# A convolution and mixture-of-experts kernel: four pairs of chunks routed together, small routing steps moved between engines, load orders fixed

## The chip, the cores and the metric

The kernel runs on one core of a Trainium2 chip. The metric is the device time of one execution in microseconds. A core has TensorE (PE: matrix products, with PEld for loading weights), VectorE (DVE), ScalarE (ACT), GpSimd (POOL) and SyncE (SP, which issues most DMA transfers here; GpSimd issues the scattered ones). Each engine runs its own list of instructions in order, and semaphores join the lists.

## The reference

```python
# x: 8 x 3584 x 192, weight_gen: 8 x 3584 x 8 heads x 7 taps, 8 experts, F = 1024
w = softmax(weight_gen, axis=-1)                       # seven taps for each row and head
y[s, head] = sum(w[s, head, k] * x_padded[s + k, head] for k in range(7))
x = y.reshape(28672, 192)
logits = x @ w_gate                                    # 28672 x 8
e = argmax(logits); g = softmax(logits)[e]
out[row] = g[row] * (relu(x[row] @ w1[e]) @ w2[e])     # each row through one expert
```

## The kernel before

The 28672 rows are cut into 28 chunks of 1024 (8 rows on each of 128 partitions). A chunk goes through these stages.

- **Convolution** (`taps`, lines 415 to 438, through `tap_ops`). VectorE multiplies the input by each of seven tap weights and adds up: seven products (`tv`, line 386) and six sums (`acc`, line 410) of 128 x 1536. For the first five chunks TensorE does the sums.
- **Split** (`high`, `low`). Each float32 row becomes a high and a low float16 part, written with its row number into a payload tile `pl` (three of them). TensorE transposes it for the gate.
- **Routing** (`finish`, lines 722 to 733). `logits` on TensorE into the PSUM tile `pm`; `route1` on VectorE (sum of the two halves `lg`, maximum, difference, one-hot `oh`; ScalarE's Exp gives `eg`); `ranks` on TensorE; `gate` (sum `se`, product with `rsx`, reciprocal into the payload); `places` (the position `pos` of each row in its expert's queue). `send` scatters the 8 rows per partition with 8 indirect DMAs of GpSimd into a queue in device memory.
- **Choice** (`choose`, `select`). As soon as a chunk is routed, a plan made ahead (`make_plan`, `t_main`) says how many tiles may be taken. `select` finds the fullest queues with seven steps on VectorE over a 1 x 72 table (`free`, `key`, `key`, `top`, `rows`, `key`, `room`). `rows` holds where each tile starts. SyncE reads it into a register.
- **Experts** (`fetch`, `experts`, `l2`). A tile has 256 rows up to chunk 4, then 384, and 128 at the end. `fetch` loads `xt` (a transposing DMA from the queue, which waits until the scatters of its chunk have landed), `wt` (the expert's weights, 1796 KB) and `meta`. For each of 8 groups TensorE makes `ph` with five matmuls (line 890), ScalarE takes the ReLU's high half `hh` (line 910), and VectorE the low half `hl` (line 913). For some tiles (those chosen up to chunk `SUBS - 1`, and every eighth from chunk 18 on) TensorE subtracts `hh` itself (line 903) and ScalarE writes `hl` (line 905). The second layer of the tile before (line 787) is mixed in between; ScalarE scales its output `o` (line 791) and GpSimd scatters it to `out`.

Tiles are numbered in the order of the choice: 0 to 13 have 256 rows, 14 is chunk 5's only tile, 15 to 17 are chunk 6's, 18 and 19 chunk 7's, and so on (31 to 33 chunk 12's, 34 and 35 chunk 13's, 47 chunk 18's first, 70 chunk 26's last).

The order of VectorE's list is written out by the program: `vector_step` (lines 1027 to 1064) keeps one clock for VectorE and one for TensorE, built from costs in the text, and puts out whatever is due: a low half, a weight step, a routing step, a split, else the next tap. A routing step that yields is due again `STEP` = 0.2 us later, so one tap usually falls between two steps. The lists of the other engines are ordered by a scheduler from what depends on what, with routing preferred. The PSUM pool of `ph` has 4 buffers, `o` has 6, `wt` 3, `xt` 3.

Of the kernel before, what the change touches and what calls it, by code (L numbers as in the profile page):

```python
# [47 lines left out]
HOLD = 6  # L48
CAPS = (128, 128, 128, 128, 112, 96, 80, 64, 48, 32)
# [4 lines left out]
FETCH = 16.0  # L54
W_AT = 10.0
# [64 lines left out]
def conv_moe_kernel(ctx: ExitStack, tc: tile.TileContext, x, wgen, w_gate, w1, w2, out):  # L120
# [43 lines left out]
    revE = const.tile([P, J, E], F32, name="revE")  # L164
    nc.gpsimd.iota(revE, pattern=[[0, J], [-1, E]], base=E, channel_multiplier=0,
# [7 lines left out]
    oh_t = []  # L173
    for i in range(2):
        t = const.tile([P, J + 1, E], F16, name=f"oh{i}")
        nc.gpsimd.memset(t, 0.0)
        oh_t.append(t)
    eg_t = []
    for i in range(2):
        t = const.tile([P, J, E + 1], F32, name=f"eg{i}")  # L180
        nc.gpsimd.memset(t[:, :, E:], 1e-9)
        eg_t.append(t)
# [270 lines left out]
    def scale(c):  # L453
        k = ch[c]
        ssq = rt.tile([P, 1], F32, name="ssq")
        nc.vector.tensor_reduce(ssq, ssqs, axis=AX.XY, op=ALU.add)  # L456
        yield 0.1
        ssi = rt.tile([P, 1], I32, name="ssi")
        nc.vector.tensor_scalar(ssi, ssq.bitcast(I32), 24, 23, op0=ALU.logical_shift_right,
                                op1=ALU.arith_shift_left)  # L460
        yield 0.1
        k.rsx = rt.tile([P, 1], F32, name="rsx", bufs=4)
# [49 lines left out]
    def logits(c):  # L512
        k = ch[c]
        k.pm = ps_m.tile([P, 512], F32, name="pm")
        k.lp = k.pm[:, 0:J * 2 * E].rearrange("p (j t e) -> p j t e", j=J, t=2)
        for j in range(J):
            for n in range(3):
                nc.tensor.matmul(k.lp[:, j], k.xg[:, 3 * j + n, :], gw[:, n], start=(n == 0), stop=(n == 2))  # L518
                clock[1] += GATE

    def route1(c):
        k = ch[c]
        k.lg = rt.tile([P, J, E], F32, name="lg")
        k.eg = eg_t[c % 2]
        nc.vector.tensor_reduce(k.lg, k.lp.rearrange("p j t e -> p j e t"), axis=AX.X, op=ALU.add)
        yield STEP
        lm = rt.tile([P, J], F32, name="lm")
        nc.vector.tensor_reduce(lm, k.lg, axis=AX.X, op=ALU.max)
        yield STEP
        nc.vector.tensor_tensor(k.lg, k.lg, lm.unsqueeze(2).to_broadcast([P, J, E]), op=ALU.subtract)  # L530
        nc.scalar.activation(k.eg[:, :, 0:E], k.lg, AF.Exp, scale=k.lsc)
        yield STEP
        pri = rt.tile([P, J, E], F32, name="pri")
        nc.vector.scalar_tensor_tensor(pri, k.lg, 0.0, revE, op0=ALU.is_ge, op1=ALU.mult)
        yield STEP
        pmx = rt.tile([P, J], F32, name="pmx")
        nc.vector.tensor_reduce(pmx, pri, axis=AX.X, op=ALU.max)
        yield STEP
        k.oh = oh_t[c % 2]
        nc.vector.tensor_tensor(k.oh[:, 0:J, :], pri, pmx.unsqueeze(2).to_broadcast([P, J, E]), op=ALU.is_equal)  # L540

    def ranks(c):
        k = ch[c]
        k.rp = k.pm[:, 256:256 + (J + 1) * E].rearrange("p (j e) -> p j e", j=J + 1)
        nc.tensor.matmul(k.rp, tri, k.oh, start=True, stop=False)
        for j in range(J):
            nc.tensor.matmul(k.rp[:, j + 1:, :], ones_h, k.oh[:, j:j + 1, :].to_broadcast([P, J - j, E]),
                             start=False, stop=(j == J - 1))
        clock[1] += 0.3

    def gate(c):
        k = ch[c]
        se = rt.tile([P, J], F32, name="se")
        nc.vector.tensor_reduce(se, k.eg, axis=AX.X, op=ALU.add)
        yield STEP
        nc.vector.tensor_tensor(se, se, k.rsx.to_broadcast([P, J]), op=ALU.mult)
        yield STEP
        nc.vector.reciprocal(k.pl.bitcast(F32)[:, :, D], se)
        yield STEP

    def places(c):
        k = ch[c]
        rk = rt.tile([P, J, E], F32, name="rk")
        bs = base[-1]
        nc.vector.tensor_tensor(rk, k.rp[:, 0:J, :], bs.unsqueeze(1).to_broadcast([P, J, E]), op=ALU.add)
        nb = rt.tile([P, E], F32, name="nb", bufs=3)
        nc.vector.tensor_tensor(nb, k.rp[:, J, :], bs, op=ALU.add)
        base.append(nb)
        yield STEP
        nc.vector.tensor_tensor(rk, rk, k.oh[:, 0:J, :], op=ALU.mult)  # L570
        yield STEP
        k.pos = rt.tile([P, J], I32, name="pos")
        with nc.allow_low_precision("queue positions are whole numbers below 2**24"):
            nc.vector.tensor_reduce(k.pos, rk, axis=AX.X, op=ALU.add)
        yield STEP

    def send(c):
        k = ch[c]
        for j in range(J):
# [18 lines left out]
    def select(T, S_, rows):  # L598
# [4 lines left out]
        nc.vector.tensor_tensor(free, room.unsqueeze(2).to_broadcast(sh), steps[T], op=ALU.add)  # L603
        yield STEP
# [10 lines left out]
        nc.vector.tensor_scalar(rows, top, -1.0, float(TOP), op0=ALU.mult, op1=ALU.add)  # L615
# [53 lines left out]
    first_ = []  # L669
    sent = [0]  # L670
# [123 lines left out]
    def fetch(n):  # L794
# [36 lines left out]
        rows_of(m)  # L831
        if n == 0:
# [6 lines left out]
    def experts():  # L839
# [25 lines left out]
        while True:  # L865
# [13 lines left out]
            for t in range(groups):  # L879
# [16 lines left out]
                if ((n % 8 == 1 and todo[n][3] >= LATE_SUBS) or todo[n][3] < SUBS) and todo[n][3] < NCH - 3:  # L896
# [236 lines left out]
```

## Time and profile before

| | |
|---|---|
| median of 3 runs | 1186.94 us (1186.53 to 1188.32) |
| profiled execution | 1185.47 us |
| its span, first to last instruction | 1183.8 us |
| mean granted TensorE clock | 0.991 |

The profile shows one execution. Busy times are the sums of listed durations; a matmul's end is modelled, and listed durations of neighbours can overlap. A wait is put down to the instruction whose semaphore came last.

### The profile page before, as it was taken

How to read it: one execution, taken by the hardware profiler on the slowest of the kernel's cores; microseconds unless marked ns; L12 is line 12 of the kernel's file. 1: busy time of each engine (PE TensorE's matmuls, PEld its weight loads, DVE VectorE, ACT ScalarE, POOL GpSimd, SP SyncE). 2: the span in 40 equal slices, each digit the busy share in tenths (PEclk: the TensorE clock that was granted, in tenths of full speed). 3: DMA queues.
4: the chain of work that ended last, by engine and by line, in shares of the span. 5: the costliest groups of instructions: out<-in, count | busy, mean ns of one | idle time of the engine just before them, and what ended most of it. 6: DMA issues, size and time to landing. Idle time of an engine off the chain costs nothing. (4 is left out here: it accounts for less than half of the span.)

```text
span 1183.8 us, 29289 instructions
## 1 busy us (share of the span) xinstructions
PE 1123.8 (95%) x11327; PEld 913.1 (77%) x11327; DVE 1034.9 (87%) x1771; ACT 647.1 (55%) x1348; POOL 696.3 (59%) x633
## 2 busy tenths in 40 slices
PE   5689799999999999999999999999999999999996
PEld 3455489998778878787788888787777777778996
DVE  7999999999999999999999999999999997833231
ACT  3555477777556555545554555656465556443342
POOL 7998647766654654664566566447555675721222
PEclk9999899999999999999999999999999999999999
DMA  9989899999889787888898788777687666799993
GB/s 280 378 299 335 248 335 308 307 307 307 254 219 279 239 257 229 258 240 232 221 290 237 209 276 260 234 209 236 235 242 245 196 151 223 235 330 353 351 344 136
DMA packets 182847, 311.44 MB, mean 263 GB/s; under 512 B 131243, under 2 KB 154785, under 8 KB 167470
## 3 DMA queue, kind: packets, MB, share of 16 engines
q1 hardware_dynamic: 160702, 264.17, 73.3%
q0 software_dynamic: 22000, 45.33, 12.0%
q8 instruction: 91, 1.49, 0.5%
q14 instruction: 54, 0.44, 0.1%
HBM read 226.97 MB, written 60.45 MB: 243 GB/s over the span
## 5 line engine op out<-in xcount | busy, mean ns | idle before, releaser
L890 PE MATMUL ph<-xt,wt 128*128 128x384 f16 (+6 forms) x3680 | 571.2, 296 | 9.5 <-DVE hl L913 5.5
L787 PE MATMUL yo<-wt,hh 128*128 128x192 f16 (+1 forms) x3648 | 489.8, 246 | 2.9 <-ACT o L791 2.9
L589 POOL DMA_INDIRECT out_dram<-o,meta x228 | 281.1, 1233 | 323.5 <-ACT o L791 254.5
L787 PE MATMUL yo<-wt,hl 128*128 128x192 f16 (+1 forms) x1824 | 438.3, 246 | 0.0
L890 PEld LDWEIGHTS <-wt 128*128 128x128 f16 x3680 | 317.7, 98 | 124.3 <-issue 6.4
L910 ACT ACTIVATE hh<-ph 128x384 f16<-128x384 f32 (+2 forms) x485 | 238.5, 495 | 292.9 <-PE ph L890 272.1
L913 DVE SCALAR_TENSOR_TENSOR hl<-ph,hh 128x384 f16<-128x384 f32 (+2 forms) x485 | 260.4, 552 | 110.7 <-ACT hh L910 110.2
L787 PEld LDWEIGHTS <-hh 128*128 128x128 f16 (+1 forms) x3648 | 330.2, 98 | 32.9 <-issue 3.7
L589 POOL DMA_INDIRECT queue<-pl,pos x224 | 289.7, 1293 | 98.6 <-issue 72.9
L386 DVE TENSOR_TENSOR tv<-x_sb,wp 128x1536 f32<-128x1536 f32 (+1 forms) x173 | 286.2, 1656 | 1.7 <-PE ph L395 1.4
L410 DVE TENSOR_TENSOR acc<-acc,tv 128x1536 f32<-128x1536 f32 x138 | 239.6, 1736 | 0.0
L787 PEld LDWEIGHTS <-hl 128*128 128x128 f16 (+1 forms) x1824 | 178.7, 98 | 18.5 <-ACT hl L905 0.2
L791 ACT ACTIVATE o<-yo,fac 128x192 f32<-128x192 f32 (+1 forms) x228 | 90.5, 418 | 89.5 <-PE yo L787 85.1
L508 ACT ACTIVATE xg<-ph 128x1024 f16<-128x1024 f16 x84 | 81.6, 1022 | 38.2 <-PE ph L506 38.0
L395 PE MATMUL ph<-tv,identf 128*128 128x384 f32 x210 | 82.6, 539 | 17.8 <-DVE tv L386 17.1
L395 PEld LDWEIGHTS ph<-tv,identf 128*128 128x128 f32 x210 | 41.4, 209 | 45.2 <-DVE tv L386 19.0
L899 ACT ACTIVATE hh<-ph 128x512 f16<-128x512 f32 (+1 forms) x88 | 48.9, 562 | 22.1 <-PE ph L890 16.0
L447 ACT ACTIVATE junk<-x_sb 128x768 bf16<-128x768 f32 (+2 forms) x56 | 48.0, 857 | 16.1 <-DVE ssq L456 6.0
L905 ACT ACTIVATE hl<-ph 128x512 f16<-128x512 f32 (+1 forms) x88 | 47.7, 559 | 10.6 <-PE ph L903 10.2
L506 PE MATMUL ph<-idh,pl 128*128 128x128 f16 x672 | 52.3, 219 | 0.4 <-DVE pl L500 0.3
L486 ACT ACTIVATE pl<-acc 128x768 f16<-128x768 f32 (+1 forms) x51 | 39.0, 805 | 15.3 <-DVE acc L410 9.2
L506 PEld LDWEIGHTS <-pl 128*128 128x128 f16 x672 | 42.7, 98 | 5.9 <-ACT pl L491 2.6
(133 smaller groups left out, 768.9 us busy)
## 6 DMA issues: line engine op xcount, KB each, us to landing
wt<-wq SPq DMA_DIRECT2D x92, 1796.0 KB
x_sb<-in_x_dram SPq DMA_DIRECT2D x27, 1344.0 KB
w_sb<-in_weight_gen_dram SPq DMA_DIRECT2D x28, 224.0 KB
wq<-ws SPq DMA_DIRECT2D x8, 772.0 KB
f<-in_moe_w_dram SPq DMA_DIRECT2D x8, 768.0 KB
f<-in_moe_w_dram SPq DMA_DIRECT2D x8, 512.0 KB
wq<-ws SPq DMA_DIRECT2D x8, 512.0 KB
wq<-ws SPq DMA_DIRECT2D x32, 128.0 KB
```

Of the source, the lines that this page charges most:

```text
L386: eng.tensor_tensor(out, xs, ws, op=ALU.mult)
L395: nc.tensor.matmul(ap[:, 0:m], identf, tf[:, 2 * i * D:2 * i * D + m], start=(n == 0), stop=(n == KW - 1))
L410: eng.tensor_tensor(ac, ac, t, op=ALU.add)
L506: nc.tensor.transpose(pt[:, m, :], p16[:, j, n * P:(n + 1) * P], idh)
L508: nc.scalar.activation(k.xg[:, i:i + 8, :], pt, AF.Copy)
L589: st = nc.gpsimd.indirect_dma_start(out=dst, out_offset=bass.IndirectOffsetOnAxis(ap=idx, axis=0), in_=src, in_offset=None, **kw)
L787: nc.tensor.matmul(y, hx[:, f, sl], w2v[:, f, t, :], start=(f == 0 and k == 0), stop=(f == NF - 1 and k == 2))
L791: nc.scalar.activation(o[0:m, :], y, AF.Copy, scale=fac[0:m, s:s + 1])
L890: nc.tensor.matmul(ph[:, g], wt[:, wc + f * P:wc + (f + 1) * P], xt[:, xc, 0:T], start=(k == 0 and g == 0), stop=(k == 4), skip_group_chec ...
L899: nc.scalar.activation(hv, ph, AF.Relu, scale=SHRINK)
L910: nc.scalar.activation(hv, ph, AF.Relu)
L913: nc.vector.scalar_tensor_tensor(lv, ph, 0.0, hv, op0=ALU.max, op1=ALU.subtract)
```

## The change

Chunks 6 and 7, 8 and 9, 10 and 11, 12 and 13 are routed together: the even chunk stops after its logits, and the odd one's `route1`, `ranks`, `gate`, `places`, `send` and `choose` handle both, on tiles of twice the width. The plan takes no tiles after the even chunk. From chunk 6 on ScalarE multiplies the gate sums by `rsx`. For selections after chunks 6 to 19 GpSimd computes `free` and ScalarE `rows`. `SUBS` falls from 6 to 5, which concerns tile 14 alone. In `fetch`, for chunks 5 to 15, `xt` is ordered on SP behind the `meta` of the tile before; for chunks 18 to 26, `wt` is issued first and `xt` behind it.

```diff
-SUBS = 6
+SUBS = 5
+ROUND = 1.2
+SMALL_TO = 20
+PAIRED = (6, 8, 10, 12)
+LATE_FROM = 18
 def t_main(c, last):
     if c < last:
-        return [T_MAIN]
+        return [] if c in PAIRED else [T_MAIN]
 def logits(c):
+        at = 0
+        if c - 1 in PAIRED:
+            k.pm, at = ch[c - 1].pm, J
+        else:
+            k.pm = ps_m.tile([P, 512], F32, name="pm")
+        k.n = at + J
...
+    def members(c):
+        return [ch[c - 1], ch[c]] if ch[c].n > J else [ch[c]]
 def route1(c):                 # all tiles [P, n, E] with n = k.n, 8 or 16
...
-        nc.scalar.activation(k.eg[:, :, 0:E], k.lg, AF.Exp, scale=k.lsc)
+        for i, m in enumerate(members(c)):
+            nc.scalar.activation(k.eg[:, i * J:i * J + J, 0:E], lg[:, i * J:i * J + J], AF.Exp, scale=m.lsc)
 def gate(c):
-        nc.vector.tensor_tensor(se, se, k.rsx.to_broadcast([P, J]), op=ALU.mult)
-        yield STEP
-        nc.vector.reciprocal(k.pl.bitcast(F32)[:, :, D], se)
-        yield STEP
+        if c > EARLY:
+            for i, m in enumerate(ms):
+                nc.scalar.activation(ss[:, i * J:i * J + J], se[:, i * J:i * J + J], AF.Copy, scale=m.rsx)
+            yield ROUND, 0.0
+        else:
+            nc.vector.tensor_tensor(ss, se, k.rsx.to_broadcast([P, J]), op=ALU.mult)
+            yield STEP
+        for i, m in enumerate(ms):
+            nc.vector.reciprocal(m.pl.bitcast(F32)[:, :, D], ss[:, i * J:i * J + J])
+            yield STEP
 def send(c):
-        for j in range(J):
-            st = scatter(queue, k.pos[:, j:j + 1], k.pl[:, j, 0:ROW // 2], "q")
+        for i, k in enumerate(members(c)):
+            for j in range(J):
+                st = scatter(queue, ch[c].pos[:, i * J + j:i * J + j + 1], k.pl[:, j, 0:ROW // 2], "q")
 def select(T, S_, rows, c):
-        nc.vector.tensor_tensor(free, room.unsqueeze(2).to_broadcast(sh), steps[T], op=ALU.add)
+        early = EARLY < c < SMALL_TO
+        eng = nc.gpsimd if early else nc.vector
+        eng.tensor_tensor(free, room.unsqueeze(2).to_broadcast(sh), steps[T], op=ALU.add)
...
+        if early:
+            nc.scalar.activation(rows, top, AF.Copy, scale=-1.0, bias=float(TOP))
+        else:
             nc.vector.tensor_scalar(rows, top, -1.0, float(TOP), op0=ALU.mult, op1=ALU.add)
 def finish(c):
         logits(c)
+        if c in PAIRED:
+            return
 def fetch(n):
-        rows_of(nc.sync.dma_start_transpose(xt[:, :, 0:T], q16[ds(r, T), 0:2 * D]))
-        nc.sync.dma_start(wt, wq[ds(e * P, P), :])
+        behind = LATE_FROM <= c < NCH - 1
+        if behind:
+            before_[:] = [nc.sync.dma_start(wt, wq[ds(e * P, P), :]).ins.name]
+        x_ = nc.sync.dma_start_transpose(xt[:, :, 0:T], q16[ds(r, T), 0:2 * D])
+        rows_of(x_)
+        if behind or PAIRED[0] - 2 < c < PAIRED[-1] + 4:
+            tc.add_manual_dep(x_.ins, before_[0], ...)      # NoSync, "order on SP"
+        if not behind:
+            nc.sync.dma_start(wt, wq[ds(e * P, P), :])
...
+        before_[:] = [m.ins.name]                           # m: the load of meta
 def experts():
-                if ((n % 8 == 1 and todo[n][3] >= LATE_SUBS) or todo[n][3] < SUBS) and todo[n][3] < NCH - 3:
+                if todo[n][3] < SUBS or (n % 8 == 1 and LATE_SUBS <= todo[n][3] < NCH - 3):
```

## Rows read from the trace of the kernel before

**Rows 1.** The profile's page, busy time of each engine in us, its share of the span and the number of instructions.

```profile
PE 1123.8 (95%) x11327; PEld 913.1 (77%) x11327; DVE 1034.9 (87%) x1771; ACT 647.1 (55%) x1348; POOL 696.3 (59%) x633
```

**Rows 2.** Busy time by stage: the stretch in us, its length, busy time (and count) of PE, PEld, DVE, ACT and POOL, granted clock, busy share of the DMA engines, GB/s.

```profile
250.00:800.00 550.00, 549.64 (x5510) 445.05 (x5509) 540.95 (x901) 314.54 (x677) 324.52 (x266) 1.00 0.85 251
800.00:1050.00 250.00, 242.44 (x2374) 191.81 (x2372) 225.66 (x424) 132.85 (x284) 151.95 (x125) 1.00 0.74 225
1050.00:1184.00 134.00, 122.23 (x1604) 113.07 (x1601) 37.57 (x61) 50.82 (x116) 31.71 (x33) 0.98 0.91 302
```

**Rows 3.** What TensorE waited for between 800 and 1050 us: us in total, times, longest.

```profile
PE ph L890 <- DVE hl L913: 4.4, 8, 1.3
PE yo L787 <- ACT o L791: 1.7, 4, 0.7
PE ph L890 <- DMA xt<-queue: 1.4, 1, 1.4
```

**Rows 4.** VectorE's timeline around the routing of chunk 11: start us, listed duration us, engine, line, operation.

```profile
383.30 0.22 DVE L554 TENSOR_REDUCE se<-eg 128x8 f32<-128x72 f32 x1
383.44 1.74 DVE L386 TENSOR_TENSOR tv<-x_sb,wp 128x1536 f32<-128x1536 f32 x1
385.10 0.55 DVE L913 SCALAR_TENSOR_TENSOR hl<-ph,hh 128x384 f16<-128x384 f32 x1
385.57 0.15 DVE L556 TENSOR_TENSOR se<-se,rsx 128x8 f32<-128x8 f32 x1
385.64 0.20 DVE L466 TENSOR_SCALAR lsc<-ssi,gofs 128x1 int32<-128x1 int32 x1
...
389.09 0.15 DVE L567 TENSOR_TENSOR nb<-pm,nb 128x8 f32<-128x8 f32 x1
389.16 0.54 DVE L913 SCALAR_TENSOR_TENSOR hl<-ph,hh 128x384 f16<-128x384 f32 x1
389.63 0.21 DVE L570 TENSOR_TENSOR rk<-rk,oh 128x64 f32<-128x64 f32 x1
389.76 0.68 DVE L364 TENSOR_REDUCE sm<-ew 128x64 f32<-128x512 f32 x1
...
399.84 0.15 DVE L615 TENSOR_SCALAR rows<-top 1x8 int32<-1x8 f32 x1
399.91 0.28 DVE L616 SCALAR_TENSOR_TENSOR key<-key,top,free 1x72 f32<-1x72 f32 x1
400.11 0.54 DVE L913 SCALAR_TENSOR_TENSOR hl<-ph,hh 128x384 f16<-128x384 f32 x1
```

**Rows 5.** Instructions by tile: duration in ns, least, median and longest, and the first and last start. First `free`, then `rk*oh`, then GpSimd's subtraction of the tap maximum; the last two lines are the long product on VectorE and the GpSimd instruction beside it in their timelines.

```profile
L603 DVE TENSOR_TENSOR free<-room,step x29: 210/211/625, 3.1 to 1010.1; 1x72 f32<-1x72 f32 x29
L570 DVE TENSOR_TENSOR rk<-rk,oh x28: 202/210/1642, 81.9 to 1004.6; 128x64 f32<-128x64 f32 x28
L351 POOL TENSOR_TENSOR w_sb<-w_sb,mx x27: 963/988/2494, 7.2 to 911.4; 128x448 f32<-128x448 f32 x27
...
717.62 1.64 DVE L570 TENSOR_TENSOR rk<-rk,oh 128x64 f32<-128x64 f32 x1
718.18 0.99 POOL L351 TENSOR_TENSOR w_sb<-w_sb,mx 128x448 f32<-128x448 f32 x1
```

**Rows 6.** ScalarE: the Exp of the routing by tile (ns, least, median, longest), and two of ScalarE's waits between 165 and 1000 us (us, times, longest).

```profile
L531 ACT ACTIVATE eg<-lg,lsc x28: 337/348/368, 73.7 to 1000.6; 128x64 f32<-128x64 f32 x28
ACT hh L910 <- PE ph L890: 220.2, 258, 3.6
ACT eg L531 <- DVE lg L530: 3.8, 5, 1.2
```

**Rows 7.** Timelines of SP and TensorE: the loads of tiles 60 to 62 as SP issues them (start, duration of the issue), and the first matmuls of tiles 15, 31 and 60.

```profile
884.92 0.33 SPq L827 DMA_DIRECT2D wt<-wq  x1
896.44 1.34 SPq L825 DMA_TRANSPOSE xt<-queue  x1
898.54 1.30 SPq L825 DMA_TRANSPOSE xt<-queue  x1
900.14 0.34 SPq L827 DMA_DIRECT2D wt<-wq  x1
901.32 4.23 SPq L825 DMA_TRANSPOSE xt<-queue  x1
...
300.05 0.49 PE L890 MATMUL ph<-xt,wt 128*128 128x384 f16 x2
509.76 0.98 PE L890 MATMUL ph<-xt,wt 128*128 128x384 f16 x5
900.35 0.81 PE L890 MATMUL ph<-xt,wt 128*128 128x384 f16 x4 [1.42 <-DMA xt<-queue]
```

**Rows 8.** GpSimd's timeline: the first scatter of chunk 7, the first and last of chunk 13, and the last scatter of chunk 23.

```profile
256.89 0.96 POOL L589 DMA_INDIRECT queue<-pl,pos  x1 [0.30 <-DVE free L603]
...
477.46 2.15 POOL L589 DMA_INDIRECT queue<-pl,pos  x1 [3.84 <-issue]
...
490.25 0.96 POOL L589 DMA_INDIRECT queue<-pl,pos  x1 [0.30 <-issue]
...
890.87 2.90 POOL L589 DMA_INDIRECT queue<-pl,pos  x1 [0.30 <-issue]
```

**Rows 9.** The page's list of DMA issues: the loads of weights and their size.

```profile
wt<-wq SPq DMA_DIRECT2D x92, 1796.0 KB
```

More of the change, by code (lines that the diff above doesn't have):

```diff
@@ L163, in conv_moe_kernel @@
     nc.vector.tensor_scalar(negi, identf, -1.0, None, op0=ALU.mult)
-    revE = const.tile([P, J, E], F32, name="revE")
-    nc.gpsimd.iota(revE, pattern=[[0, J], [-1, E]], base=E, channel_multiplier=0,
+    revE = const.tile([P, E], F32, name="revE")
+    nc.gpsimd.iota(revE, pattern=[[-1, E]], base=E, channel_multiplier=0,
                    allow_small_or_imprecise_dtypes=True)
@@ L172, in conv_moe_kernel @@
     nc.vector.tensor_scalar(room, base0[0:1, :], -1.0, float(TOP), op0=ALU.mult, op1=ALU.add)
-    oh_t = []
-    for i in range(2):
-        t = const.tile([P, J + 1, E], F16, name=f"oh{i}")
+    oh_t, eg_t = [], []
+    for i in range(3):
+        t = const.tile([P, (1 + i // 2) * J + 1, E], F16, name=f"oh{i}")
         nc.gpsimd.memset(t, 0.0)
         oh_t.append(t)
-    eg_t = []
-    for i in range(2):
-        t = const.tile([P, J, E + 1], F32, name=f"eg{i}")
+        t = const.tile([P, (1 + i // 2) * J, E + 1], F32, name=f"eg{i}")
         nc.gpsimd.memset(t[:, :, E:], 1e-9)
@@ L461, in scale @@
         yield 0.1
-        k.rsx = rt.tile([P, 1], F32, name="rsx", bufs=4)
+        if c - 1 in PAIRED:
+            k.rsx = ch[c - 1].rsx2[:, 1:2]
+        else:
+            k.rsx2 = rt.tile([P, 2], F32, name="rsx", bufs=4)
+            k.rsx = k.rsx2[:, 0:1]
         nc.vector.tensor_scalar(k.rsx.bitcast(I32), ssi, -1.0, float(197 << 23), op0=ALU.mult, op1=ALU.add)
@@ L513, in logits @@
         k = ch[c]
-        k.pm = ps_m.tile([P, 512], F32, name="pm")
-        k.lp = k.pm[:, 0:J * 2 * E].rearrange("p (j t e) -> p j t e", j=J, t=2)
+        at = 0
+        if c - 1 in PAIRED:
+            k.pm, at = ch[c - 1].pm, J
+        else:
+            k.pm = ps_m.tile([P, 512], F32, name="pm")
+        k.n = at + J
+        k.lp = k.pm[:, 0:k.n * 2 * E].rearrange("p (j t e) -> p j t e", j=k.n, t=2)
         for j in range(J):
             for n in range(3):
-                nc.tensor.matmul(k.lp[:, j], k.xg[:, 3 * j + n, :], gw[:, n], start=(n == 0), stop=(n == 2))
+                nc.tensor.matmul(k.lp[:, at + j], k.xg[:, 3 * j + n, :], gw[:, n], start=(n == 0), stop=(n == 2))
@@ L545, in ranks @@
         nc.tensor.matmul(k.rp, tri, k.oh, start=True, stop=False)
-        for j in range(J):
-            nc.tensor.matmul(k.rp[:, j + 1:, :], ones_h, k.oh[:, j:j + 1, :].to_broadcast([P, J - j, E]),
-                             start=False, stop=(j == J - 1))
-        clock[1] += 0.3
+        for j in range(n):
+            nc.tensor.matmul(k.rp[:, j + 1:, :], ones_h, k.oh[:, j:j + 1, :].to_broadcast([P, n - j, E]),
+                             start=False, stop=(j == n - 1))
+        clock[1] += 0.3 * n / J
@@ L561, in places @@
+        if c > EARLY:
[8 more added lines that the diff above has]
+            yield STEP
     def places(c):
         k = ch[c]
-        rk = rt.tile([P, J, E], F32, name="rk")
+        n = k.n
@@ L564, in places @@
+        sh = [P, n, E]
+        rk = rt.tile(sh, F32, name="rk", padded_shape=[P, 2 * J, E])
         bs = base[-1]
[L565 removed]
+        nc.vector.tensor_tensor(rk, k.rp[:, 0:n, :], bs.unsqueeze(1).to_broadcast(sh), op=ALU.add)
         nb = rt.tile([P, E], F32, name="nb", bufs=3)
[L567 removed]
+        nc.vector.tensor_tensor(nb, k.rp[:, n, :], bs, op=ALU.add)
@@ L568, in places @@
         base.append(nb)
         yield STEP
-        nc.vector.tensor_tensor(rk, rk, k.oh[:, 0:J, :], op=ALU.mult)
+        nc.vector.tensor_tensor(rk, rk, k.oh[:, 0:n, :], op=ALU.mult)
         yield STEP
-        k.pos = rt.tile([P, J], I32, name="pos")
+        k.pos = rt.tile([P, n], I32, name="pos", padded_shape=[P, 2 * J])
         with nc.allow_low_precision("queue positions are whole numbers below 2**24"):
@@ L595, in scatter, with select @@
         return st
-    def select(T, S_, rows):
+    def select(T, S_, rows, c):
         bs = base[-1]
@@ L684, in choose @@
                 else:
-                    yield from select(T, m, rows)
+                    yield from select(T, m, rows, c)
                 for i in range(m):
```

47 lines of the change are left out of this document (28 added, 19 removed).

## The prediction

> **What bounds the kernel now.** I read the busy times first. TensorE and VectorE are both nearly full, GpSimd and ScalarE are not [rows 1]. An average hides stages, so the table by stage came next. From 250 to 800 us TensorE is busy 549.64 of 550 us and VectorE 540.95: two engines full at once. From 800 to 1050 us TensorE drops to 242.44 of 250, so it stands idle 7.56 us; after that VectorE has little left and TensorE works off the last tiles alone. The granted clock is 1.00, the 2.4 GHz level, up to 1050 us and 0.98 after it [rows 2]. The waits of TensorE between 800 and 1050 us say whom it misses: 4.4 us for the low halves `hl` that VectorE writes (line 913, they free PSUM), 1.7 us for ScalarE's `o`, 1.4 us for an `xt` that landed late [rows 3].
>
> I read this as one story. VectorE does convolution, routing and low halves, and has more to do per chunk than TensorE. TensorE starts with a stock of tiles already chosen, eats it up to 800 us without a gap, and then runs at VectorE's pace. So a microsecond taken off VectorE between 200 and 960 us should come off the end, up to the 7.56 us that TensorE now stands idle; a microsecond off TensorE alone is worth little there, since it is the one waiting.
>
> **The parts, in VectorE time.** A listed duration overlaps the next start by about 0.08 us, so I price an instruction from its start to the next one's [rows 4]: `tv` 1.66 (383.44 to 385.10), a low half 0.47 (389.16 to 389.63), `rk*oh` 0.13 (389.63 to 389.76), `se` 0.14, `nb` 0.07, the gate product 0.07 (385.57 to 385.64), `rows` 0.07, the last `key` 0.20. `lg` reads twice the elements of the others; 64 more cost 0.07 (below), so 0.20.
> - Pairs. Eleven route instructions of chunks 6, 8, 10 and 12 go: 0.20 for `lg`, 0.07 for `nb`, 0.14 for `se`, and eight of about 0.13, in sum 1.44. The partner's grow. From 64 to 1536 elements the price rises from 0.13 to 1.66, 1.04 ns an element; 64 more are 0.067, `lg` takes 128 more, so 11 times 0.067 = 0.74. Net 0.70. Reciprocals stay. One `select` goes too: five of 0.14, `rows` 0.07, `key` 0.20, 0.97. Together 1.67 a pair, 6.7 for four.
> - The gate product moves to ScalarE for chunks 6 to 26: 21 times 0.07 = 1.5.
> - `free` to GpSimd and `rows` to ScalarE in ten selections (7, 9, 11, 13, 14 to 19): 10 times 0.21 = 2.1.
> - SUBS 5 gives the one tile of chunk 5 back to VectorE: 8 low halves of 0.47, plus 3.8. TensorE loses 8 matmuls of 384 columns; four such took 0.81 listed, 0.16 each net [rows 7], so 1.3 less. The wider rank matmuls of a pair have 1224 columns for 720; at 0.16 per 384, 0.2 a pair, 0.8 for four. TensorE nets 0.5 less. The late tiles (n = 49, 57, 65) keep their subtraction.
> - Sum for VectorE: 6.7 + 1.5 + 2.1 - 3.8 = 6.5 less.
>
> **What the change adds.**
> - GpSimd sums beside VectorE. A product `rk*oh`, 0.21 normally, once took 1.64, and a `free` once 0.62 against 0.21 [rows 5]; both happened beside GpSimd's `w_sb` subtraction, 0.99 long (the first of the two at 718.18). A GpSimd `free` of 72 elements is not in the trace: it is at most as long as `w_sb`, so ten cost VectorE 0 to 9.9. Excess 1.43 and 0.41 over 27 `w_sb` is 0.07 each; I take 0.1, so 1.0. The Trainium skill, page "SBUF — State Buffer", section "Who interferes with whom", says that a VectorE instruction with two SBUF inputs and a GpSimd one that reads SBUF exclude each other for a whole instruction. The two long rows agree. By that rule alone, each `free` costing a full block of 0.99, the sum would turn from 6.5 less into 3.4 more.
> - The reciprocal now waits for ScalarE, and every instruction behind it on VectorE (taps, low halves) with it; TensorE then waits for PSUM. The nearest rows: ScalarE's Exp of the same routing takes 0.35 and itself sat waiting five times; a ScalarE instruction ahead of it can wait up to 3.6 for TensorE [rows 6]. The planner allows 1.2. Bounds 0 and 17 times 3.6 = 61; the taps planned between cover most, so I take 0.5 for all. ScalarE gets some 31 short instructions beside its 55% [rows 1].
> - Sixteen scatters in a row. Eight for chunk 13 run from 477.46 to 491.21, and the `out` scatters queue behind them [rows 8]; sixteen take 27 us. Six `o` buffers cover about two tiles, as long as that: 0, up to some 4 if `o` is held once. The pair's first `xt` may start only after the last scatter. Tile 31 is hit hardest: scatters from about 476 to 503, its `xt` 2.7 us after the end, as it was for tile 60 (893.77 to 896.44), near 506, while its first matmul was at 509.76 [rows 7, 8]. Cost 0 to 8 (if its weights queue behind `xt` on SP; 1796 KB at that stretch's 251 GB/s are 7 us, an estimate [rows 2, 9]); for tile 60 SP issued the weights first, so I am near the low end and take 0.5. Tiles 15, 20 and 26 of the other pairs lie further behind their scatters: for chunk 7 those began at 256.89, sixteen end near 284, and tile 15 starts at 300.05 [rows 7, 8].
> - Orders on SP. Up to chunk 15 `xt` goes behind the last `meta`, about where it is now: 0. From chunk 18, `wt` goes first. For the first tile of a selection it does so already (884.92, then 896.44) [rows 7]. For the others see the second rival; I take 0.3.
> - In sum 2.3 more, so VectorE nets 4.2 less. That lies under the 7.56 bound. The profiled execution, 1185.47, would become 1181.3; the median of the runs shown is 1.5 higher, 1186.94, and becomes **1182.7**.
>
> **Rivals.**
> - *Nothing reaches the end.* TensorE is full to 800 us, and only 4.4 of its later waits name VectorE; if the waits for `o` and `xt` grow as VectorE's shrink, or the ScalarE round and the long bursts eat the 4 us, what is left is TensorE's 0.5: 1186.4. For it: the small margin of 4.2 over costs bounded far higher. Against: VectorE is over 97% busy in the same stretch, so its work sets when chunks are chosen.
> - *Slower: the transposes behind the weights.* From chunk 18 on, each `xt` stands on SP behind its own `wt`, which waits for a buffer. An `xt` issued with nothing ahead took 1.30 on SP; one issued 1.2 us after a `wt` took 4.23 [rows 7]. Of 24 tiles 15 are not first of a selection. If 4 of them start 2.9 late the sum is 11.6 - 4.2 = 7.4 more: 1194.3. It decides from about 6.6 us of stalls, two to three such tiles. Against: `wt` leads its first matmul by 15.4 for tile 60. The Trainium skill, "DMA: Bandwidth & Descriptors", section "Queues, rings and completion order", says that each DMA engine takes descriptors in ring order, so a transpose would wait for all of the weights; the 4.23 row is of that kind.
> - *A GpSimd `free` behind the burst* is the same sign: VectorE's `key` would wait up to 24 us. But its inputs are ready a chunk ahead, so I give it 0.03, inside the slower case.
> - *The change does less than it says:* the SP orders up to chunk 15 are those of today; counted at 0 above.
>
> **How the numbers follow.** Forecast 0.55, nothing 0.25, slower 0.20. A measurement here tells about 0.2%, 2.4 us, from no change. The forecast's case is faster by more than that nine times in ten; 0.04 comes from the edge of the second case. So faster 0.54, same 0.27, slower 0.19. Low end: all 7.56 idle and the 0.5 gone and a us for the runs' spread, 1177.9, say 1177.5. High end: the second rival's price, 1194; beyond lie a late `free` or `wt` at many tiles.
>
> **What would show it.** In the changed profile: VectorE with 105 instructions fewer (72 by the pairs, 21 products, 20 of the selections, 8 more low halves) and a listed busy time some 15 us less (6.5, and 0.08 for each); four routings with 128x128 tiles; TensorE idle in 800 to 1050 us down from 7.56 to about 3; `lg` and `pos` of chunk 20 some 4 us earlier. Wrong if VectorE shows waits for ScalarE at the reciprocal or for GpSimd at `key` of over 3 us in sum, if TensorE waits at tile 31, or if waits for `xt` appear after chunk 18.

## The result, and the profile after

The changed kernel takes 1196.37 us (median of 6 runs, 1192.84 to 1197.55), the kernel before 1186.99 in the same session: ratio 1.0074, 95% interval 1.0059 to 1.0089. It is slower by some 9 us, on the other side of the forecast and above its range. The profiled execution is the fastest of the six, 1192.84 us with a span of 1191.1, so it holds 7.3 us of the loss. Its page and its table by stage, in the columns of [rows 1, 2]:

```profile
PE 1127.5 (95%) x11315; PEld 913.5 (77%) x11315; DVE 1034.2 (87%) x1665; ACT 649.1 (54%) x1372; POOL 673.4 (57%) x645
```

```profile
250.00:800.00 550.00, 541.78 (x5389) 435.95 (x5388) 534.15 (x815) 310.85 (x683) 318.62 (x280) 1.00 0.83 248
800.00:1050.00 250.00, 247.35 (x2427) 196.47 (x2425) 226.66 (x421) 136.69 (x297) 146.59 (x127) 1.00 0.76 228
1050.00:1191.00 141.00, 128.56 (x1659) 117.90 (x1656) 39.82 (x65) 52.86 (x121) 33.09 (x35) 0.99 0.92 301
```

The idle time that the forecast aimed at did shrink: TensorE stands 2.65 us in 800 to 1050 instead of 7.56. But in 250 to 800, where it had stood 0.36 us, it now stands 8.22. At 1050 us it has 6.3 us more left to do (128.56 against 122.23). The loss is made early, in a stretch in which I had expected none.

What TensorE waits for between 250 and 400 us (us in total, times, longest):

```profile
PE ph L939 <- DMA wt<-wq: 3.9, 2, 3.3
```

One wait of 3.3 us is most of the 4.6 us that TensorE stands idle in this stretch. The other 3.6 of the 8.22 us lie between 400 and 800 us, mostly in eight short waits for `hl` (3.2 us in sum). The long wait is in front of tile 15, the first tile of the pair of chunks 6 and 7. SP's list around it, first after, then before (start, us; in the list before, the transpose at 281.90 is already tile 16's, tile 15's own was issued at 272.63, right behind tile 14's):

```profile
277.59 0.34 SPq L875 DMA_DIRECT2D wt<-wq  x1
288.37 0.38 SPq L878 DMA_DIRECT2D meta<-queue  x1
289.09 1.32 SPq L868 DMA_TRANSPOSE xt<-queue  x1
290.52 0.52 SPq L344 DMA_DIRECT2D x_sb<-in_x_dram  x1
291.33 0.33 SPq L875 DMA_DIRECT2D wt<-wq  x1
```

```profile
277.74 0.38 SPq L830 DMA_DIRECT2D meta<-queue  x1
280.23 0.34 SPq L342 DMA_DIRECT2D x_sb<-in_x_dram  x1
281.90 3.44 SPq L825 DMA_TRANSPOSE xt<-queue  x1
285.63 0.35 SPq L827 DMA_DIRECT2D wt<-wq  x1
```

Before, tile 15's weights are issued at 285.63, 14.4 us ahead of its first matmul at 300.05 [rows 7]. After, at 291.33, because SP stood from 278 to 288 in front of tile 14's small `meta`. SP's own wait for such a buffer in 255 to 300, after and then before, and GpSimd's list after:

```profile
SPq L878 <- DMA out_dram<-o,meta: 15.2, 3, 10.2
```

```profile
SPq L830 <- DMA out_dram<-o,meta: 1.0, 2, 0.7
```

```profile
282.54 0.96 POOL L620 DMA_INDIRECT queue<-pl,pos  x1 [0.30 <-issue]
283.81 0.99 POOL L620 DMA_INDIRECT out_dram<-o,meta  x1 [0.30 <-ACT pl L492]
285.10 1.23 POOL L620 DMA_INDIRECT out_dram<-o,meta  x1 [0.30 <-issue]
286.32 0.30 POOL L636 TENSOR_TENSOR free<-room,step 1x72 f32<-1x72 f32 x1
```

Read backwards: SP wants a `meta` buffer; there are four; each is read, as the index, by the `out` scatters of its tile; these stand on GpSimd behind the pair's sixteen scatters, the last of which is issued at 282.54. TensorE then does this (start, us; below it the stage table for two short stretches):

```profile
300.02 0.33 PE L826 MATMUL yo<-wt,hh 128*128 128x192 f16 x2
303.64 1.78 PE L939 MATMUL ph<-xt,wt 128*128 128x384 f16 x5 [3.29 <-DMA wt<-wq]
```

```profile
303.00:307.00 4.00, 3.36 (x14) 2.05 (x15) 2.57 (x8) 0.49 (x1) 0.00 (x0) 0.57 1.07 386
307.00:312.00 5.00, 5.00 (x55) 3.84 (x53) 4.57 (x8) 2.54 (x7) 0.72 (x1) 1.00 0.68 200
```

Five matmuls that take 0.98 us otherwise [rows 7] take 1.78: behind the idle stretch the granted clock is at the 1.2 GHz level for 3.4 us. The kernel before shows no such drop between 142 and 1178 us.

### The profile page after: what moved, and what is told of

Same layout as the page of the kernel before. It is cut to its first block, busy times and chain, and to the rows that moved or that the text cites. A ratio compares the mean times of both kernels' runs of the same rounds, so it can differ in the third digit from the quotient of the medians.

```text
span 1191.1 us, 29184 instructions
## 1 busy us (share of the span) xinstructions
PE 1127.5 (95%) x11315; PEld 913.5 (77%) x11315; DVE 1034.2 (87%) x1665; ACT 649.1 (54%) x1372; POOL 673.4 (57%) x645
## 4 chain that ended last, share of the span: by engine, by line
PE 61%; DVE 13%; DMA 10%; issue 7%; POOL 4%; ACT 2%; SPq 0%; POOLq 0%; DVEq 0%; ACTq 0%
PE ph L939 28%; PE yo L826 27%; DMA wt<-wq 5%; DVE tv L388 3%; DVE hl L962 3%; DVE acc L412 3%; PE ph L512 2%; DMA xt<-queue 2%; POOL out_dram L620 2%; PE ph L952 1%; PE ph L397 1%; DMA wq<-ws 1%; PE pm L530 1%; ACT xg L514 1%; DMA f<-in_moe_w_dram 1%
## 5 line engine op out<-in xcount | busy, mean ns | idle before, releaser
L620 POOL DMA_INDIRECT out_dram<-o,meta x228 | 262.8, 1153 | 353.1 <-ACT o L830 267.5
L959 ACT ACTIVATE hh<-ph 128x384 f16<-128x384 f32 (+2 forms) x493 | 242.6, 496 | 279.3 <-PE ph L939 259.4
L962 DVE SCALAR_TENSOR_TENSOR hl<-ph,hh 128x384 f16<-128x384 f32 (+2 forms) x493 | 266.9, 557 | 120.3 <-ACT hh L959 120.0
L620 POOL DMA_INDIRECT queue<-pl,pos x224 | 278.8, 1245 | 103.0 <-issue 77.5
L948 ACT ACTIVATE hh<-ph 128x512 f16<-128x512 f32 (+1 forms) x80 | 45.0, 567 | 22.2 <-PE ph L939 18.2
L954 ACT ACTIVATE hl<-ph 128x512 f16<-128x512 f32 (+1 forms) x80 | 44.4, 566 | 11.0 <-PE ph L952 10.6
```

Of the source, the lines that this page charges most:

```text
L620: st = nc.gpsimd.indirect_dma_start(out=dst, out_offset=bass.IndirectOffsetOnAxis(ap=idx, axis=0), in_=src, in_offset=None, **kw)
L959: nc.scalar.activation(hv, ph, AF.Relu)
L962: nc.vector.scalar_tensor_tensor(lv, ph, 0.0, hv, op0=ALU.max, op1=ALU.subtract)
```

## The experiments

Theory A: a pair's sixteen scatters hold the `out` scatters back, through them buffers and SP, and so stall tile 15. B: the weights ahead of the transposes from chunk 18 on. C: the pairs' steps in VectorE's own list. D: the fixed order of `xt` behind `meta`. Every ratio is against the kernel before in the same job (1185.8 to 1186.4 us, save in the last two jobs); 0.1% is 1.19 us.

**Undoing one part of the change.**

e1, ten `meta` buffers (the memory comes from `rows`):
```diff
-meta = px.tile([P, 4, 2], F32, name="meta", bufs=AHEAD + 1 if ring else 4)
+meta = px.tile([P, 4, 2], F32, name="meta", bufs=AHEAD + 1 if ring else 10)
-rows = rt.tile([1, 8], I32, name="rows", bufs=40)
+rows = rt.tile([1, 8], I32, name="rows", bufs=30)
```


> The changed kernel with ten buffers for meta in place of four (and 30 for rows in place of 40, to make room); nothing else. Theory A: the sixteen scatters hold back the out scatters, those hold the meta buffers, SyncE waits up to 10.2 us for one and issues the weights of tile 15 late, TensorE stands still at 300 us and its clock falls, and VectorE, whose list is fixed, loses its lead with it. Then the wait on meta goes, tile 15 starts by 300, and the time falls from 1196 to 1186 to 1189. Theory B, the weights ahead of the transposes from chunk 18 on cost the time: stays at 1194 to 1198. Theory C, the pairs cost it in VectorE's own plan, not through SyncE: stays at 1193 to 1198 although the wait on meta is gone.

e2, no pairs:
```diff
-PAIRED = (6, 8, 10, 12)
+PAIRED = ()
-        if behind or PAIRED[0] - 2 < c < PAIRED[-1] + 4:
+        if behind:
```


> The changed kernel without the pairs and without the fixed order on SP for chunks 5 to 15; the moved steps, SUBS 5 and the weights first from chunk 18 on stay. Theory A and theory C: no burst of sixteen, so no stall at tile 15; VectorE keeps 1.5 + 2.1 us of saving against 3.8 more, so about the time of before, 1185 to 1189. Theory B: stays at 1194 to 1198.

e3, no fixed order for chunks 5 to 15 (the second edit of e2 alone):


> The changed kernel without the fixed order of xt behind the meta of the tile before, chunks 5 to 15. Theory A: the wait on meta stays and holds SyncE all the same, but the transposes may pass it; a part comes back, 1190 to 1196. If the order itself is the cause (theory D): 1186 to 1189. Theories B and C: 1194 to 1198.

e4, weights behind the transposes to the end (`LATE_FROM = 28`):


> The changed kernel with the weights behind the transposes from chunk 18 on, as before the change (LATE_FROM = 28); nothing else. Theory A, C and D: unchanged, 1194 to 1198, and the same stall at 300 us. Theory B: 1186 to 1189.

Measured: e1 1.0026 [1.0011, 1.0041]; e2 1.0138 [1.0113, 1.0164]; e3 1.0090 [1.0065, 1.0115]; e4 1.0074 [1.0046, 1.0102].

e1 gives back 0.48%, 5.7 us, with the stall and the low clock at 300 gone: A holds for the larger part, but not in the size that it was given. e1 came at 1190.67 us, above A's 1186 to 1189 and below the ranges of B and C, and tile 15 did not start by 300. In e4 and e3 a stall for `wt` stays before 310 us (3.7 and 5.7), so neither B nor D makes it. e3 (1198.2 us) missed too, above every range that it was given: no part comes back, and the transposes wait up to 8.4 us for the scatters there. e1's SP waits in 255 to 300, and tile 15's start:

```profile
SPq L868 <- DMA queue<-pl,pos: 7.6, 1, 7.6
```

```profile
301.32 0.99 PE L939 MATMUL ph<-xt,wt 128*128 128x384 f16 x5 [0.69 <-DMA wt<-wq]
```

No wait for `meta` is left, but tile 15's own transpose waits for the sixteenth scatter, its weights stand behind it on SP, and the tile still starts 1.27 us later than before. In the full change it starts 3.6 us later. So the four `meta` buffers account for 2.3 us of its delay and for the 1.7 us of the low clock behind it; 1.3 us stay with ten buffers, from the burst itself. The rest of the 9 us is not settled by e1 (its profile is of the slowest of its twelve runs, 1193.18 us): TensorE is busy 542.09 us of 250 to 800, as in the full change, now with many small waits (`hl` 3.5 us in 9, `wt` 2.3, `o` 1.5).

e2 is a miss for every theory: without the pairs the change is slower still, 16 us. TensorE's waits between 880 and 930 us there:

```profile
PE ph L939 <- DVE hl L962: 7.4, 1, 7.4
PE ph L939 <- DMA xt<-queue: 4.8, 1, 4.8
```

VectorE is 7 us late by chunk 20 (below), and near tile 60 TensorE finds rows and PSUM late. So what the pairs take off VectorE is needed as long as VectorE is behind.

**Undoing parts with ten buffers.** Each starts from e1. f1: `SUBS = 6`. f2: the gate product on VectorE. f3: `SMALL_TO = 0`. f4: all three and `LATE_FROM = 28`, so that pairs and their order are all that is left of the change. f2's edit:
```diff
-        if c > EARLY:
+        if False:
...
+            if n > J:
+                nc.vector.tensor_tensor(ss.rearrange("p (t j) -> p t j", t=2), se.rearrange("p (t j) -> p t j", t=2),
+                                        ms[0].rsx2.unsqueeze(2).to_broadcast([P, 2, J]), op=ALU.mult)
```


> The kernel with ten meta buffers, and chunk 5's tiles subtract on TensorE again (as in the kernel before); all else of the change stays. It stands at a ratio of 1.0026 (about 4 us over before) without this edit. Theory S (what is left of the loss is VectorE's: chunk 5's subtractions come to it just where its lead is made, and the conversion goes from 3.7 us ahead at chunk 10 to 1.1 us behind at chunk 11): the jump of 4.8 us between chunks 10 and 11 shrinks to about 1, TensorE's small waits between 250 and 800 fall from 14 us to under 8, ratio 0.999 to 1.001. Rival G (the gate product's way over ScalarE and the place that it has in VectorE's order cost it): nothing of this changes but TensorE works about 1.5 us more, ratio 1.002 to 1.005. Rival F (GpSimd's row of free places holds VectorE up): the same as G.

> The kernel with ten meta buffers, and the gate product is made by VectorE in every chunk (one operation for a pair), so nothing is asked of ScalarE between the sum and the reciprocal; all else of the change stays. Theory G: the waits that came with the way over ScalarE go, and with them 2 us or more, ratio 0.999 to 1.001. Theory S and rival F: VectorE gets some 1.5 us of work back and nothing is won, ratio 1.002 to 1.004.

> The kernel with ten meta buffers, and free places and row numbers are VectorE's again in every chunk; all else of the change stays. Theory F (an operation of GpSimd beside VectorE's sums of two inputs makes one of the two wait, up to 2 us each, some 14 times): ratio 1.000 to 1.002. Theories S and G: VectorE gets 2.1 us back, ratio 1.003 to 1.005.

> The kernel with ten meta buffers, and of the change only the pairs of chunks and the order of SP for chunks 5 to 15 are left: gate product, free places and row numbers are VectorE's, chunk 5's tiles subtract on TensorE, and the weights are loaded behind the transposes to the end. If the pairs give VectorE the 6.7 us that were forecast for them and these reach the end through TensorE's idle time behind 800: ratio 0.995 to 0.998 (1181 to 1184). If a pair's steps, twice as long, hold the second halves of the tiles up and TensorE loses that in small waits between 250 and 800 (rival C): ratio 1.001 to 1.003, with those waits near the 14 us of the kernel with ten meta buffers.

Measured: f1 1.0058 [1.0046, 1.0070]; f2 1.0071 [1.0055, 1.0087]; f3 1.0089 [1.0067, 1.0110]; f4 1.0008 [0.9997, 1.0018].

No theory called f1 to f3: each part undone alone is slower than e1, all undone together is level with the kernel before, so the parts do not add up. f2 and f3 do not isolate their parts, since a new stall at 425 us covers them: TensorE and ScalarE in 400 to 450 us of f2,

```profile
PE yo L830 <- ACT o L834: 4.6, 1, 4.6
```

```profile
ACT o L834 <- DMA out_dram<-o,meta: 6.8, 2, 5.5
```

It is A at a later pair and with the other buffer: the `out` scatters behind the sixteen of chunks 10 and 11 (390.4 to 417.2 us in f2) also hold the six `o` buffers, and ScalarE cannot write. f3 shows the same with 5.2 us. The prediction had this wait, "up to some 4 if `o` is held once", and put it at 0. In f1 TensorE stands 4.6 us for `xt` near 1030, with the clock at its low level for 6.8 us after it.

f4 is level with the kernel before, between the two expectations. VectorE's lead is there: the tap weights `wp` of chunk 20 (before, f4, the full change, e2; start, us):

```profile
686.87 0.66 DVE L374 SCALAR_TENSOR_TENSOR wp<-ew,rsx,sm 128x448 f32<-128x448 f32 x1
```

```profile
676.90 0.67 DVE L376 SCALAR_TENSOR_TENSOR wp<-ew,rsx,sm 128x448 f32<-128x448 f32 x1
```

```profile
685.96 0.68 DVE L376 SCALAR_TENSOR_TENSOR wp<-ew,rsx,sm 128x448 f32<-128x448 f32 x1
```

```profile
693.79 0.67 DVE L376 SCALAR_TENSOR_TENSOR wp<-ew,rsx,sm 128x448 f32<-128x448 f32 x1
```

f4 is 10.0 us ahead, the full change 0.9, e2 6.9 behind. And f4's lead does not arrive. Its stage table, then its last tiles and those of the kernel before:

```profile
250.00:800.00 550.00, 546.93 (x5462) 441.86 (x5461) 541.99 (x853) 316.80 (x676) 343.61 (x276) 1.00 0.87 254
800.00:1050.00 250.00, 246.72 (x2429) 196.40 (x2427) 221.43 (x416) 134.45 (x288) 141.68 (x123) 1.00 0.75 224
```

```profile
1156.11 1.60 PE L943 MATMUL ph<-xt,wt 128*128 128x80 f16 x40
...
1168.22 0.29 PE L943 MATMUL ph<-xt,wt 128*128 128x32 f16 x4 [3.28 <-SPq L1161]
```

```profile
1157.98 1.60 PE L890 MATMUL ph<-xt,wt 128*128 128x80 f16 x40
...
1167.18 0.27 PE L890 MATMUL ph<-xt,wt 128*128 128x32 f16 x4 [1.46 <-SPq L1108]
```

The view names SyncE's closing line, which stands behind the last load; what tile 91 waits for is the last weight load itself. Tile 88 starts 1.87 us earlier than before; tile 91 starts 1.04 later. Both kernels issue the last weights 17 us ahead of it (1150.0 before, 1151.0 in f4), and between 1050 and 1150 the DMA engines are busy throughout (340 GB/s in f4, 345 before). This suggests theory E: the stream of the last weights sets the end. A second loss follows the longer wait. The stage table for 1167 to 1173 us, before and then f4:

```profile
1167.00:1173.00 6.00, 5.45 (x88) 5.11 (x89) 0.43 (x1) 1.37 (x4) 0.92 (x1) 1.00 0.05 13
```

```profile
1167.00:1173.00 6.00, 4.78 (x49) 4.47 (x50) 0.00 (x0) 0.42 (x1) 0.00 (x0) 0.50 0.01 4
```

Behind f4's 3.28 us of idle time the clock stays at the 1.2 GHz level for 6.8 us, behind the 1.46 us of the kernel before it stays at 2.4 GHz. From the start of tile 91 to the last tile's second layer f4 takes 8.0 us, the kernel before 6.0. So 2.0 us go to the clock, whatever makes the wait.

**Third job.** g1 is f1 with `LATE_FROM = 28`, and so f4 plus the three small moves; g2 is e2 with `LATE_FROM = 28`. g3 (from f4) and g4 (from the full change, four buffers) break up the burst:
```diff
 for i, k in enumerate(members(c)):
+    if i:
+        yield PAUSE                      # 10.0
     for j in range(J):
         st = scatter(queue, ...)
+        if i:
+            tc.add_manual_dep(st.ins, last_o[0], ..., reason="order on POOL")
```


> The kernel with ten meta buffers and chunk 5's subtractions on TensorE (ratio 1.0058, TensorE standing 4.7 us at 1028 for the transposed rows of tile 69, with the clock at 0.5 for 6.8 us behind it), and now the weights are loaded behind the transposes to the end, as in the kernel before. Against the kernel with pairs only it keeps the gate product on ScalarE, free places on GpSimd and row numbers on ScalarE. Theory B (with the weights first, a transpose waits in SP's order until a weight buffer is free, and that is too late for tile 69 once the other losses are gone): the 4.7 us and the low clock go, ratio 0.998 to 1.001. Rival (the rows of tile 69 are late because of the scatters ahead of them on GpSimd): the stall stays, ratio 1.004 to 1.007.

> The change without pairs (ratio 1.0138, with TensorE standing 5.0, 7.6, 2.2 and 2.4 us at 903, 917, 1039 and 1053), and now also with the weights loaded behind the transposes to the end. What is left of the change is the gate product on ScalarE, free places on GpSimd, row numbers on ScalarE, and chunk 5's subtractions on VectorE. Theory B: the four stalls are the weights' place ahead of the transposes; they go, with the low clock behind three of them, ratio 1.001 to 1.005. Rival (VectorE, 7 us behind from chunk 11 on without the pairs, finds the rows of tiles 60 to 70 too late whatever SP does): the stalls stay in most part, ratio 1.009 or more.

> The kernel with pairs only and ten meta buffers (ratio 1.0008), and a pair's sixteen scatters are issued as eight, then the output scatters that have come up by then (one to three), then eight. Theory A (the sixteen in a row hold back the output scatters and through them the buffers): TensorE's waits between 250 and 350, 4.5 us against 0.6 in the kernel before, fall to 2 or less, ratio 0.995 to 0.999. Rival (the second eight, some 4 us later, make the rows of the pair's tiles late): TensorE waits for transposed rows at the first tiles of chunks 7, 9, 11 or 13, ratio 1.002 or more.

> The full change with its four meta buffers, and a pair's sixteen scatters are issued as eight, then the output scatters that have come up by then (one to three), then eight; nothing else. Theory A (the burst itself, by the order of GpSimd's queue, is the cause; buffers are only where it is felt): the stall before tile 15 (3.5 us and the low clock) goes as it did with ten buffers, ratio 1.001 to 1.004. Rival (four buffers are too few for the pairs, in whatever order): the stall stays, ratio 1.006 to 1.009.

Measured: g1 1.0038 [1.0025, 1.0051]; g2 1.0075 [1.0061, 1.0089]; g3 1.0016 [1.0002, 1.0030]; g4 1.0061 [1.0048, 1.0075].

- g1, g2 and g3 came between their two expectations; g4 came in its rival's range, though not by the rival's mechanism.
- g1 against f1: B shows there, by 0.20%, with intervals that just overlap and from two different jobs; the `xt` wait near 1030 falls from 4.6 to 1.6 (a `wt` wait of 2.1 appears) and the low clock goes.
- g2 against e2: of the four stalls the two near 1040 and 1053 shrink to 1.0 and 1.5 us (and name `hl` and `wt`), the two near 903 and 920 stay (3.8 and 8.9): half B, half VectorE's lateness.
- g1 against f4: the three moves, worth 3.6 us in the forecast, cost 0.30%, 3.6 us, with intervals apart. VectorE's waits between 160 and 1000 us, f4 and then g1:

```profile
DVE hl L966 <- ACT hh L963: 7.1, 11, 3.5
```

```profile
DVE hl L962 <- ACT hh L959: 19.8, 17, 3.2
```

VectorE stands 12.7 us more in front of low halves whose high half is not made yet; other waits fall, so that its waits grow by 9.2 us in all (17.0 to 26.2). The moves change the costs in the hand-made list, and the list puts those low halves where TensorE has not come to. That the list is the cause is my reading; no run held the list and moved the work.
- g4: the `meta` wait is gone from SP's list, yet tile 15 waits 3.7 us for its weights: the split ends the sixteenth scatter some 2 us later, its transpose waits 10.0 us for that, and the weights follow. A second stall, 6.1 us for `xt` at 1044, is like f1's. g3 gains nothing either. Splitting the burst this way is no cure; the first tile of a pair needs all sixteen. SP's wait in 255 to 300 us of g4 and TensorE's in 255 to 330:

```profile
SPq L877 <- DMA queue<-pl,pos: 16.5, 2, 10.0
```

```profile
PE ph L948 <- DMA wt<-wq: 3.7, 1, 3.7
```

**The last six runs.** h1 (f4) and h2 (the kernel before) leave out every second load of the last weights:
```diff
+again = late and n - lates[1] >= 8 and (n - lates[1]) % 2 == 1
-wt = pw.tile([P, WROW], F16, name="wt")
+wt = kept[0] if again else pw.tile([P, WROW], F16, name="wt")
...
-        if not behind:
+        if not behind and not again:
             nc.sync.dma_start(wt, wq[ds(e * P, P), :])
```
In h2, which has no `behind`, the load stands under `if not again`.
h3 is the three moves alone on the kernel before; h4 is f4 with four `meta` buffers; h5 and h6 are h1 and h2 again.

> Pairs only with ten meta buffers (ratio 1.0008), and from the ninth tile of the last chunk's stretch on every second tile multiplies with the weights of the tile ahead of it and loads none of its own (some 7 of the last 16 loads of 1796 KB are left out, so these tiles' results are not the reference's). Theory E (the end is set by the stream of the last weights: tile 91 starts when its weights land, at 1167.15 in the kernel before and 1168.20 in this one without the edit, though TensorE is 1.9 us ahead at tile 88): TensorE's waits behind 1150 (7.7 us with those that the low clock makes) fall under 2, and the 1.9 us of lead arrive: ratio 0.993 to 0.996, 2 to 3 us under that of the kernel before with the same edit. Rival (the lead is lost elsewhere): ratio as that of the kernel before with the same edit, within 1 us.

> The kernel before, and from the ninth tile of the last chunk's stretch on every second tile multiplies with the weights of the tile ahead of it and loads none of its own (these tiles' results are not the reference's). Theory E: tile 91 no longer waits for its weights, the 1.6 us before it go, ratio 0.997 to 0.999. Rival: the wait of tile 91 has another cause and stays, ratio 0.999 to 1.001.

> The kernel before with only the small moves of the change: the gate product on ScalarE behind chunk 5, free places on GpSimd and row numbers on ScalarE for chunks 6 to 19; no pairs, chunk 5 subtracts on TensorE, weights behind the transposes, four meta buffers. If these moves are the 3.6 us of VectorE's time that were forecast and VectorE's time is worth what was forecast: ratio 0.997 to 0.999. Theory E (VectorE's time is worth nothing at the end): 0.999 to 1.001. If they cost by themselves (VectorE waits for the engines that it asks, or GpSimd's operations hold it up): 1.002 or more, and then VectorE is behind the kernel before at chunk 20.

> Pairs only, with the four meta buffers of the change (the same kernel with ten is at 1.0008). Theory A (sixteen scatters in a row hold the output scatters, these the meta buffers, these SP): TensorE stands 3 us or more before tile 15, with the low clock behind it, ratio 1.004 to 1.007. Rival (the buffers bind only together with the rest of the change): no such stall, ratio 1.000 to 1.002.

> Once more the kernel with pairs only, ten meta buffers, and every second tile of the last chunk's stretch from the ninth on without a load of weights of its own (it multiplies with those of the tile ahead of it, so these tiles' results are not the reference's). Theory E (the stream of the last weights sets the end and takes VectorE's lead back): ratio 0.993 to 0.996, 2 to 3 us under the kernel before with the same edit, and no wait of TensorE over 1 us behind 1150. Rival (the lead is lost elsewhere): within 1 us of the kernel before with the same edit.

> Once more the kernel before with the same edit in its last stretch (results of these tiles are not the reference's). Theory E: the 1.6 us in which tile 91 waits for its weights go, ratio 0.997 to 0.999. Rival: the wait stays, ratio 0.999 to 1.001.

Measured: h1 1.0080 [1.0045, 1.0116], h2 1.0003 [0.9975, 1.0031], h3 1.0168 [1.0124, 1.0212], h4 1.0163 [1.0121, 1.0205]; h5 1.0224 [1.0125, 1.0322], h6 1.0066 [1.0018, 1.0114]. In these two jobs the kernel before itself took 1285 and 1303 us (medians) instead of 1186. TensorE's waits in 250 to 1050 us of h2 show what was different:

```profile
PE yo L787 <- issue: 12.5, 15, 1.4
PE pm L518 <- issue: 7.1, 12, 1.2
PE ph L506 <- issue: 6.8, 12, 1.1
```

"Issue" means that TensorE waits for nothing that the profile shows. In the kernel before in the first session the whole list of that stretch sums to 7.8 us and has no such line. In that condition not even h3 and h4, which load all weights, wait for the last ones, so theory E was not decided, twice; h3's ratio too is not carried over. With the same edit the pairs lose 0.8% there (h1 against h2) and 1.6% (h5 against h6), so that f4 is level holds for the first condition alone. Pairs with four buffers (h4) against ten (h1) lose another 0.8%. That ratio is thin, since equal edits came out 0.6% (h2, h6) and 1.4% (h1, h5) apart between the two jobs. The traces carry the point. h4's waits near tile 15, SP's in 255 to 320 and TensorE's in 255 to 330:

```profile
SPq L882 <- DMA out_dram<-o,meta: 22.5, 2, 20.7
```

```profile
PE ph L943 <- DMA wt<-wq: 10.7, 1, 10.7
```

In h1 SP has no such wait for `out_dram`, and TensorE's longest wait for `wt` is 0.7 us. So in that condition the pairs alone, with the buffers that they were given, make the stall; the rest of the change is not needed for it. Its size is not carried over.

No version beat the kernel before; f4 comes level with it.

## Why the prediction was wrong

1. **Sixteen scatters in a row: the step that failed.** It was priced at 0.5 us and placed at tile 31, and of tiles 15, 20 and 26 it was said that they lie further behind their scatters. Tile 31 shows no wait for its rows or weights, but that says little: its `xt` was issued at 505.41, where 506 was forecast, and TensorE reached it 8.8 us later than before, at 518.54. Tile 15 stands 3.3 us, with 1.7 us more at the low clock behind it, and ten buffers in place of four give back 5.7 us (e1). Two things were left out. The first was in the text itself: the rule used for tile 31, that `xt` starts 2.7 us after the last scatter and the weights may stand behind it, gives for tile 15 about 284 + 2.7, then 2.5 us on SP, then 12 us for the weights (e1: 289.37 to 301.32; 12.3 in the full change), thus 301, not under 300.05. The prediction's 7 us for a weight load, its size over the rate of the stretch, leaves these 12 out. The second was a buffer: I counted the `o` buffers that `out` scatters hold, and not the four `meta` buffers that they hold as well. With ten buffers 1.3 of tile 15's 3.6 us of delay stay, so the larger part is the second.
2. **"Orders on SP up to chunk 15: 0"** holds: e3 is no better than the full change.
3. **"A microsecond taken off VectorE comes off the end, up to 7.56": the premise that failed beside it.** It fails on the gaining side. f4 puts VectorE 10 us ahead at chunk 20 and cuts the late idle time to 3.28 us, and comes level. Part of it went to TensorE's waits in 250 to 800, where f4 stands idle 3.07 us against 0.36. The rest is lost in the last tiles: from tile 88 to 91, by some 2.9 us, and then 2.0 us at the low clock. That the stream of the last weights sets this I read off the tiles, which wait for weights in both kernels; the runs meant to show it did not decide it. On the losing side VectorE's time does count (e2).
4. **VectorE's sum, 6.5 less.** The instructions came out (106 fewer, 105 forecast: 22 products moved, not 21), the 8 added low halves too (493 against 485). The sign "listed busy time some 15 us less" was mis-stated. The page's busy time counts overlapping durations once (the listed durations sum to 1157.9 us before, the page has 1034.9), so the 0.08 of each instruction does not come off it: the forecast in the page's measure was 6.5 less, and it fell by 0.7. The sum of the listed durations, for which 15 was right, fell by 2.2: low halves (2.6 us beyond the eight) and sums of two inputs (2.1) took longer, a set-up step before 165 us too (2.7), and some 5 us are spread and stay open. At chunk 20 VectorE is 0.9 us ahead by `wp`, by `lg` 0.3 behind and by `pos` 1.3 ahead, instead of 4. The pairs' own term is not too large: f4 is 10 us ahead at chunk 20, with 6.7 forecast. The moves' 3.6 has the wrong sign (g1 against f4).
5. **`free` on GpSimd** was priced at 1.0 with a bound of 9.9. Seven of the ten ran 0.30 us, three 1.56, 1.63 and 1.97, and VectorE never waited for their result. The three fell beside VectorE's sum `acc` of two inputs, and GpSimd was the one that waited (the three, then the sum beside the second):

```profile
428.64 1.63 POOL L636 TENSOR_TENSOR free<-room,step 1x72 f32<-1x72 f32 x1
509.05 1.97 POOL L636 TENSOR_TENSOR free<-room,step 1x72 f32<-1x72 f32 x1
662.70 1.56 POOL L636 TENSOR_TENSOR free<-room,step 1x72 f32<-1x72 f32 x1
```

```profile
509.11 1.75 DVE L412 TENSOR_TENSOR acc<-acc,tv 128x1536 f32<-128x1536 f32 x1
```

The sum is no longer than usual (1.75 us). The Trainium skill, "SBUF — State Buffer", "Who interferes with whom", makes the two exclude each other; the trace agrees on that, and the price lay with GpSimd in these three. Four of the seven short ones fell beside VectorE's product `tv`, whose weights `wp` lie in PSUM.

6. **The reciprocal's wait on ScalarE**: 0.4 us once, 0.5 taken. Right.
7. **The slower rival, transposes behind weights**: not what happened. Undone in the full change it changes nothing (e4). It shows where less else is late: weakly in f1 against g1, and in half of e2's stalls. I had the sign's chance at 0.19 with the wrong mechanism, and the range ended at that rival's price.

What stays open: the some 3 to 4 us of the loss that ten buffers do not give back, whether the last weights set the floor, and why the moves make VectorE's low halves wait.

## What to carry to other kernels

When work is gathered into a longer burst on an in-order queue, list everything that stands behind it and every buffer that this holds, then follow each buffer to the queue that asks for it; the first tile of the batch waits for the whole burst, and what is queued behind its load waits with it. A microsecond of the fuller engine is worth a microsecond only until the next bound, so look for that bound at the end of the program before valuing a saving. Where a planner makes the lists, a moved cost can reorder the rest (not shown here by a run of its own), and single parts need not add up (f1 to f4).

## What the runs showed that was not expected

- A stall costs more than its idle time: 3.3 us idle before tile 15, then 3.4 us at the 1.2 GHz level, 1.7 us more; in f4 3.28 us idle before tile 91, then 6.8 us at that level, 2.0 us more.
- A small sum on GpSimd took 0.30 us, and up to 1.97 beside a VectorE sum with two inputs in SBUF; beside a VectorE product with one input in PSUM it stayed at 0.30.
